# Down projection over 512 tokens with a collected remainder, weight work in both stages, and one split tile of 576 columns per SiLU product

## The chip, the cores and the metric

One core of one Trainium2 chip. The metric is device time in microseconds (us), a median over runs. The kernel before takes 1488.43 us, the median of 3 runs that lie between 1488.2 and 1488.91.

## The reference

Three layers follow one another over 8 batches of 576 tokens, 4608 tokens in all, with a model width of 512.

```python
def sm_attn(qq, kk, vv):
    s = scale * np.matmul(qq, kk.transpose(0, 1, 3, 2))
    ...
    return np.matmul(a, vv)
p_packed = sm_attn(p, k, v)          # 32 packed rows for each head
out = sm_attn(q, p_packed, p_packed)
...
g = x @ w_gate                       # first MLP: 512 -> 1536 -> 512
silu = g * (1.0 / (1.0 + np.exp(-g)))
return (silu * (x @ w_val) @ w_out)
...
h = x @ w_in                         # second MLP: 512 -> 2048 -> 512
return (h * np.cos(h)) @ w_out
```

The attention has 8 heads of 64. Everything is float32 at the interface. The kernel gets near that with pairs: a value is split into a rounded part "hi" and the remainder "lo", both of the 4-byte type f32r, and a product is three matmuls, hi x hi, hi x lo and lo x hi (the list PASSES).

## The kernel before, in words

**Stages.** A block is one batch of 576 tokens. For each of eight blocks there is an up stage (`a_up`, L402 to L448) and a down stage (`a_down`, L478 to L499) of the first MLP. The attention of the next block runs in pieces between the matmul groups of the down stage. The second MLP follows over all 4608 tokens, from DRAM (`x2d`), in its own stage of 384 and 512 columns (L685, L700).

**Up stage.** It has 12 tiles f of 128 hidden units, and for each two halves c of 288 tokens. A half of blocks 1 to 7 has 12 matmuls of 288 columns into the banks `pg` and `pv` (L433). ScalarE takes SiLU of `pg` (L441), VectorE multiplies with `pv` into a tile `h` of 288 columns (L444), and a half later the product is split: ScalarE writes the hi part, VectorE the lo part of `g` (helper `split`, L86 and L87). The stationary operand `wp` is the gate and value weight already multiplied with the packed rows of the attention; its first four tiles are made and split in the down stage before (`a_wp`, step 6), so that the up stage's first matmuls wait for that split. In block 0 the up stage decodes weights of the first MLP as well.

**Down stage.** It has eight groups n = (o, c) of 36 matmuls of 288 columns: output tile o, token half c, 12 tiles f and three passes. Each group accumulates in one bank, which ScalarE evicts to `x2e` (L498) and sends to `x2d` by a DMA from its own queue (L499). Ahead of groups 0, 2, 3, 4, 5 and 6 stand the pieces of the next block's attention: `a_s1` (scores of the packed rows, with their softmax), `a_t` (transposes), `a_pp`, `a_ppt`, `a_s2` (second scores, with the softmax in two chains u of 576 columns) and `a_wp`.

**Weight work.** The weights of the second MLP come in a packed form. In blocks 1 to 6 each half of the up stage carries one step of their preparation (`extra`, L450 to L464): load, decode on ScalarE and VectorE, sums, a split, and a store to DRAM (`w2_load`, `w2_decode`, `w2_work`, `w2_store`). That makes 24 steps a block.

**Order.** The kernel is written under a manual schedule: each engine executes its instructions in the order in which the code issues them, and SP and ScalarE each issue DMAs in that order too. An engine that waits holds all that is queued behind it. Tiles come from pools with a fixed number of buffers: `ct` 18, `mt` 12, `ht` 11, and eight PSUM banks.

Of the kernel before, what the change touches and what calls it, by code (L numbers as in the profile page):

```python
# [22 lines left out]
NPAIR = H // 2  # L23
HS = S // 2
NC = -(-S // 128)
SPAD = 128 * NC
# [3 lines left out]
NG = NPF // 2  # L30
SBUFS, CBUFS = 11, 18
SIN_SCALE = 6.28318500518798828
# [8 lines left out]
def attention_mlp_kernel(ctx: ExitStack, tc: tile.TileContext, qT, kT, vP, pP, wgv, w1o, w2, out):  # L41
# [12 lines left out]

    x2d = dr.tile([KD, 128, NT], F32, name="x2d")
    w2u = dr.tile([NPF, 7, 128, 512], F32, name="w2u")
    w2d = dr.tile([NF2, 128, 2, 512], F32, name="w2d")
# [10 lines left out]
    def mt(shape, dt, name):  # L68
        return sb.tile(shape, dt, tag="m", name=name, bufs=12)

    def ht(shape, dt, name):
        return sb.tile(shape, dt, tag="s", name=name, bufs=SBUFS)
# [325 lines left out]
    def flush_split():  # L398
        while pend_split:
            pend_split.pop(0)()  # L400

    def a_up(b):  # L402
        g = []
        for f in range(NF1):
# [9 lines left out]
            if b == 0:  # L414
                for u in range(2):
                    for c in range(2):
                        for o, p_ in zip((0, 128), banks[c]):
                            PE.matmul(  # L418
                                out=p_, lhsT=w[:, u, o:o + 128], rhs=a2[u][:, HS * c:HS * c + HS],
                                start=(u == 0), stop=(u == 1),  # L420
                            )
                    if u == (f == 0) and f + 1 < NF1:
                        a_wp0(f + 1)
            for c in range(2):
                sl = slice(HS * c, HS * c + HS)
# [16 lines left out]
                flush_split()  # L442
                h_ = ht([128, HS], F32, "h")
                DVE.tensor_tensor(out=h_, in0=s_, in1=pv, op=ALU.mult)  # L444
                pend_split.append(lambda h_=h_, gt=gt, sl=sl: split(h_, gt[:, 0, sl], gt[:, 1, sl]))
                extra(b, f, c)
            prefetch(b, f)
        return g  # L448

    def extra(b, f, c):  # L450
        if b == 0:
            u_step(0, 1)
            u_step(1, 1)
            if f == 0:
                u_step(2, 1)
        elif b < B - 1:
            s_ = 24 * (b - 1) + 2 * f + c
            if s_ % 2 == 0 and s_ // 2 < 4 * NF2:
                w2_store()
                w2_load(s_ // 2 + 1)  # L460
                w2_work(2)
                w2_decode(s_ // 2)
            else:
                w2_work(1)  # L464

    def prefetch(b, f):
# [7 lines left out]
        if f == 9 and b == 0:  # L474
            for j in range(NPAIR):
                load_v(n, j)

    def a_down(b, g, steps):  # L478
        for n in range(8):
            for s_ in steps.get(n, ()):  # L480
                s_()
            if 0 < b < B - 1 and n == 0:
                for j in range(NPAIR):
                    load_v(b + 1, j)
            if b + 1 < B and n == (2 if b == 0 else 0):
                for j in range(NPAIR):
                    load_q(b + 1, j)
            o, c = n // 2, n % 2
            sl = slice(HS * c, HS * c + HS)
            acc = bank([128, HS], "o1")  # L490
            for f in range(NF1):
                for i, (x, y) in enumerate(PASSES):
                    PE.matmul(  # L493
                        out=acc, lhsT=wo[o, f // 4][:, x, f % 4, :], rhs=g[f][:, y, sl],
                        start=(f == 0 and i == 0), stop=(f == NF1 - 1 and i == 2),
                    )
            ev = ht([128, HS], F32, "x2e")
            ACT.activation(out=ev, in_=acc, func=AF.Copy)  # L498
            ACT.dma_start(out=x2d[o, :, S * b + HS * c:S * b + HS * c + HS], in_=ev)  # L499

# [51 lines left out]
    with tc.manual_schedule():  # L552
# [38 lines left out]
        for b in range(B):  # L591
# [4 lines left out]
            if b == 0:  # L596
                w2_load(0)
            n = b + 1
            steps = {}
# [239 lines left out]
```

## Time and profile before

| | before |
|---|---|
| median of 3 runs | 1488.43 us |
| profiled execution | 1488.04 us |
| its span, first to last instruction | 1486.3 us |
| TensorE matmuls busy | 1478.3 us, 99% |
| VectorE busy | 985.8 us, 66% |
| ScalarE busy | 839.4 us, 56% |
| granted TensorE clock, mean | 1.000 |
| DMA, mean over the span | 173 GB/s |

The span lies inside the profiled execution's time; 1.7 us stand around it. The down stages of the eight blocks begin at 83.5, 172.3, 260.8, 349.4, 437.6, 525.6, 613.5 and 700.2 us; the second MLP's stage begins at 738.4 us. PE means matmuls and PEld the loading of their stationary operands, which lies beside them. Matmuls are pipelined: the mean time of one in the profile is from its start to its end, and the next starts before that end.

### The profile page before, as it was taken

Reading aid. Unit: us, or ns where it says so; the run is one execution under the profiler, and the core shown is the slowest. Engines: PE = TensorE matmul, PEld = TensorE weight load, DVE = VectorE, ACT = ScalarE, POOL = GpSimd, SP = SyncE. Lnnn points to the kernel's source line nnn. Section 1 sums busy time; section 2 is a strip of 40 time slices with the busy share of each in tenths; the row PEclk is TensorE's granted clock in tenths of the full one; section 3 lists DMA queues with packets and bytes.
Section 4 is the critical chain, followed back from the end, with each engine's and each line's share of the span. In section 5 each row is a group of like instructions: output and inputs, shape, how many; then the busy total and the mean of one; then the engine's idle time right before and its main releaser. Section 6 shows DMA issues by size and latency. Waiting matters only on the chain.

```text
span 1486.3 us, 27615 instructions
## 1 busy us (share of the span) xinstructions
PE 1478.3 (99%) x10476; PEld 1338.7 (90%) x10476; DVE 985.8 (66%) x2048; ACT 839.4 (56%) x1917; POOL 3.0 (0%) x22
## 2 busy tenths in 40 slices
PE   9999999999999999999999999999999999999999
PEld 6689998999899998989989999999999999999997
DVE  6988749485673837355286866776686686677654
ACT  6986737375572736434284645656555564565642
POOL 0000000000000000000000000000000000000000
PEclk9999999999999999999999999999999999999999
DMA  8742616355162542201295586576667558556641
GB/s 328 260 156 86 239 46 226 117 173 195 52 194 75 161 136 89 80 22 43 92 393 178 181 288 197 178 241 204 215 191 256 180 180 290 195 179 195 206 161 43
DMA packets 129411, 257.14 MB, mean 173 GB/s; under 512 B 13568, under 2 KB 37120, under 8 KB 129280
## 3 DMA queue, kind: packets, MB, share of 16 engines
q1 hardware_dynamic: 120064, 245.94, 50.4%
q10 hardware_dynamic: 9216, 9.44, 1.8%
q8 instruction: 83, 1.36, 0.4%
q14 instruction: 48, 0.39, 0.1%
HBM read 213.39 MB, written 41.94 MB: 172 GB/s over the span
## 4 chain that ended last, share of the span: by engine, by line
PE 95%; DVE 2%; ACT 2%; DMA 1%; issue 0%; SPq 0%; ACTq 0%; DVEq 0%
PE acc L700 26%; PE p L685 23%; PE o L493 20%; PE pg L433 9%; PE pv L433 9%; PE wp L386 3%; PE pg L418 1%; PE pv L418 1%; PE pp L203 1%; PE s L229 1%; PE s L151 1%; PE wp L371 0%; DMA qt<-in_qT 0%; PE tp L192 0%; DMA vt<-in_vP 0%
## 5 line engine op out<-in xcount | busy, mean ns | idle before, releaser
L700 PE MATMUL acc<-wd,g 128*128 128x512 f32 x1728 | 413.8, 389 | 0.0
L685 PE MATMUL p<-xs,up 128*128 128x384 f32 x2016 | 372.9, 337 | 1.3 <-ACT p L760 1.3
L700 PEld LDWEIGHTS acc<-wd,g 128*128 128x128 f32 x1728 | 322.4, 188 | 57.1
L685 PEld LDWEIGHTS p<-xs,up 128*128 128x128 f32 x2016 | 353.7, 188 | 12.7 <-ACT p L760 1.6
L493 PEld LDWEIGHTS o<-g,wo 128*128 128x128 f32 x2304 | 306.7, 188 | 13.8 <-DVE d L250 5.0
L493 PE MATMUL o<-g,wo 128*128 128x288 f32 x2304 | 316.6, 296 | 0.3 <-DVE wo L87 0.2
L663 ACT ACTIVATE t<-c,quarter 128x384 f32<-128x384 f32 x144 | 88.4, 614 | 196.7 <-DVE c L773 191.0
L433 PE MATMUL pg<-a,wp 128*128 128x288 f32 x1008 | 162.4, 296 | 0.0
L433 PE MATMUL pv<-a,wp 128*128 128x288 f32 x1008 | 160.6, 294 | 0.0
L433 PEld LDWEIGHTS pg<-a,wp 128*128 128x128 f32 x1008 | 142.4, 188 | 11.7 <-ACT wp L86 8.4
L433 PEld LDWEIGHTS pv<-a,wp 128*128 128x128 f32 x1008 | 143.0, 188 | 0.0
L87 DVE TENSOR_TENSOR g<-h,g 128x288 fp32r<-128x288 f32 x192 | 87.5, 456 | 39.4 <-ACT g L86 39.2
L673 DVE TENSOR_TENSOR g<-t,g 128x384 fp32r<-128x384 f32 x192 | 106.0, 552 | 8.0 <-ACT g L660 7.8
L665 DVE TENSOR_TENSOR t<-t,k 128x384 f32<-128x384 f32 x192 | 106.1, 552 | 3.5 <-ACT k L669 1.8
L768 DVE TENSOR_TENSOR u<-v,p 128x384 f32<-128x384 f32 x48 | 26.6, 554 | 118.2 <-PE p L685 117.9
L441 ACT ACTIVATE silu<-pg 128x288 f32<-128x288 f32 x192 | 78.3, 408 | 42.0 <-PE pg L433 37.5
L666 ACT ACTIVATE t<-t 128x384 f32<-128x384 f32 x192 | 98.2, 512 | 2.6 <-DVE t L665 2.5
L498 ACT ACTIVATE x2e<-o 128x288 f32<-128x288 f32 x64 | 26.5, 413 | 128.3 <-PE o L493 127.9
L660 ACT ACTIVATE g<-t 128x384 fp32r<-128x384 f32 x192 | 98.5, 513 | 0.4 <-DVE t L671 0.4
L86 ACT ACTIVATE g<-h 128x288 fp32r<-128x288 f32 x192 | 85.0, 443 | 24.2 <-DVE h L444 23.8
L669 ACT ACTIVATE k<-t 128x384 int32<-128x384 f32 x192 | 98.2, 511 | 0.0
L444 DVE TENSOR_TENSOR h<-silu,pv 128x288 f32<-128x288 f32 x192 | 86.0, 448 | 16.1 <-PE pv L433 5.9
(95 smaller groups left out, 1346.9 us busy)
## 6 DMA issues: line engine op xcount, KB each, us to landing
up<-w2u SPq DMA_DIRECT2D x336, 256.0 KB, 3.2
wd<-w2d SPq DMA_DIRECT2D x96, 512.0 KB, 6.2
raw<-in_w SPq DMA_DIRECT2D x64, 256.0 KB, 3.2
w2u<-w2p SPq DMA_DIRECT2D x56, 256.0 KB, 2.2
raw<-in_wgv SPq DMA_DIRECT2D x24, 512.0 KB, 7.5
vt<-in_vP SPq DMA_DIRECT2D x32, 320.0 KB, 4.3
kt<-in_kT SPq DMA_DIRECT2D x32, 288.0 KB, 5.0
qt<-in_qT SPq DMA_DIRECT2D x32, 288.0 KB, 6.0
```

The source lines that it names most:

```text
L87: eng.tensor_tensor(out=lo, in0=src, in1=hi.bitcast(F32), op=ALU.subtract)
L433: PE.matmul(out=p_, lhsT=w[u][:, x, o:o + 128], rhs=a2[u][:, y, sl], start=(n == 0), stop=(n == 5),)
L444: DVE.tensor_tensor(out=h_, in0=s_, in1=pv, op=ALU.mult)
L493: PE.matmul(out=acc, lhsT=wo[o, f // 4][:, x, f % 4, :], rhs=g[f][:, y, sl], start=(f == 0 and i == 0), stop=(f == NF1 - 1 and i == 2),)
L660: ACT.activation(out=three["g"][:, 0, :], in_=three["t"], func=AF.Copy)
L663: ACT.activation(out=now["t"], in_=now["h"], func=AF.Identity, scale=1.0 / TWO_PI, bias=quarter)
L665: DVE.tensor_tensor(out=one_["t"], in0=one_["t"], in1=one_["k"], op=ALU.subtract)
L666: ACT.activation(out=one_["t"], in_=one_["t"], func=AF.Sin, scale=SIN_SCALE)
L669: ACT.activation(out=now["k"], in_=now["t"], func=AF.Copy)
L673: DVE.tensor_tensor(out=three["g"][:, 1, :], in0=three["t"], in1=three["g"][:, 0, :].bitcast(F32), op=ALU.subtract)
L685: PE.matmul(out=out, lhsT=w[:, u, 128 * k:128 * k + 128], rhs=x[:, v, k, :], start=(first and k == 0 and i == 0), stop=(last and k == 1 an ...
L700: PE.matmul(out=acc, lhsT=gs[p, a, t][:, x, o:o + 128], rhs=wd[j, f][:, y, :], start=(f == 0 and n == 0), stop=(f == 3 and n == 2),)
```

## The change

**The down stage** takes tokens 0 to 511 of a block in four groups of 36 matmuls of 512 columns (`down_group`), instead of eight groups of 36 of 288. The attention's pieces stand at the same eighths of the stage as before, which are now the beginnings and the middles of the groups. An accumulator is evicted in two halves of 256 columns, each with its own DMA.

**The remainder.** The last 64 tokens of a block's `g`, hi and lo, are stored to DRAM (`rest`), 24 transfers of 128 x 64 a block on SP's queue, in the down stage behind the first half group; in block 7 they are stored along the up stage. The collected strips of the eight blocks make one more window of 512 columns. It is loaded back in 24 transfers of 128 x 512 (`load_rest`) and multiplied by `a_rest` in front of block 7's own down stage.

**Weight steps.** Of a block's 24 steps 16 stay in the up stage (two of three halves) and eight move into the down stage, two in each group, ahead of the tiles f = 3 and f = 9.

**The SiLU product** of a tile f is one tile `h` of 576 columns in blocks 1 to 7, written in halves and split once a tile instead of twice. Block 0 is as before. The pools become `ht` 9 and `mt` 13.

```diff
@@ -22,13 +22,15 @@
 ...
 HS = S // 2
+WIN = 512
+REST = S - WIN
 NC = -(-S // 128)
 SPAD = 128 * NC
 TH = 384
 NCH = NT // (2 * TH)
 NPF = NF2 // 2
 NG = NPF // 2
-SBUFS, CBUFS = 11, 18
+SBUFS, CBUFS = 9, 18
 SIN_SCALE = 6.28318500518798828
 
 PI = float(np.pi)
@@ -53,6 +55,7 @@
     dr = ctx.enter_context(tc.tile_pool(name="dr", bufs=1, space=bass.MemoryType.DRAM))
 
     x2d = dr.tile([KD, 128, NT], F32, name="x2d")
+    rest = dr.tile([NF1, 2, 128, B, REST], F32, name="rest")
     w2u = dr.tile([NPF, 7, 128, 512], F32, name="w2u")
     w2d = dr.tile([NF2, 128, 2, 512], F32, name="w2d")
 
@@ -66,7 +69,7 @@
         return sb.tile(shape, dt, tag="c", name=name, bufs=CBUFS)
 
     def mt(shape, dt, name):
-        return sb.tile(shape, dt, tag="m", name=name, bufs=12)
+        return sb.tile(shape, dt, tag="m", name=name, bufs=13)
 
     def ht(shape, dt, name):
         return sb.tile(shape, dt, tag="s", name=name, bufs=SBUFS)
@@ -399,6 +402,8 @@
         while pend_split:
             pend_split.pop(0)()
 
+    gr = []
+
     def a_up(b):
         g = []
         for f in range(NF1):
@@ -421,6 +426,7 @@
                             )
                     if u == (f == 0) and f + 1 < NF1:
                         a_wp0(f + 1)
+            hw = mt([128, S], F32, "h") if b > 0 else None
             for c in range(2):
                 sl = slice(HS * c, HS * c + HS)
                 pg, pv = banks[c]
@@ -440,12 +446,32 @@
                 s_ = ht([128, HS], F32, "silu")
                 ACT.activation(out=s_, in_=pg, func=AF.Silu)
                 flush_split()
-                h_ = ht([128, HS], F32, "h")
+                h_ = hw[:, sl] if b > 0 else ht([128, HS], F32, "h")
                 DVE.tensor_tensor(out=h_, in0=s_, in1=pv, op=ALU.mult)
-                pend_split.append(lambda h_=h_, gt=gt, sl=sl: split(h_, gt[:, 0, sl], gt[:, 1, sl]))
+                if b == 0:
+                    pend_split.append(lambda h_=h_, gt=gt, sl=sl: split(h_, gt[:, 0, sl], gt[:, 1, sl]))
+                elif c == 1:
+                    pend_split.append(lambda h_=hw, gt=gt: split(h_, gt[:, 0], gt[:, 1]))
                 extra(b, f, c)
             prefetch(b, f)
+            if b == B - 1 and f > 0:
+                store_rest(b, f - 1, g[f - 1])
+                if f > 2:
+                    gr.append(load_rest(f - 3))
         return g
+
+    w2_n = [0]
+
+    def w2_step():
+        s_ = w2_n[0]
+        w2_n[0] += 1
+        if s_ % 2 == 0 and s_ // 2 < 4 * NF2:
+            w2_store()
+            w2_load(s_ // 2 + 1)
+            w2_work(2)
+            w2_decode(s_ // 2)
+        else:
+            w2_work(1)
 
     def extra(b, f, c):
         if b == 0:
@@ -453,15 +479,8 @@
             u_step(1, 1)
             if f == 0:
                 u_step(2, 1)
-        elif b < B - 1:
-            s_ = 24 * (b - 1) + 2 * f + c
-            if s_ % 2 == 0 and s_ // 2 < 4 * NF2:
-                w2_store()
-                w2_load(s_ // 2 + 1)
-                w2_work(2)
-                w2_decode(s_ // 2)
-            else:
-                w2_work(1)
+        elif b < B - 1 and (2 * f + c) % 3 < 2:
+            w2_step()
 
     def prefetch(b, f):
         n = b + 1
@@ -475,28 +494,68 @@
             for j in range(NPAIR):
                 load_v(n, j)
 
+    def store_rest(b, f, gt):
+        for i in range(2):
+            SP.dma_start(out=rest[f, i, :, b, :], in_=gt[:, i, WIN:S].bitcast(F32))
+
+    def load_rest(f):
+        if f < NF1 // 2:
+            r = [mt([128, B, REST], F32R, "gr") for _ in range(2)]
+        else:
+            both = ct([128, 2, B, REST], F32R, "gr")
+            r = [both[:, i] for i in range(2)]
+        for i in range(2):
+            SP.dma_start(out=r[i].bitcast(F32), in_=rest[f, i])
+        return r
+
+    def down_group(o, moving, steps, to, between=None):
+        acc = bank([128, WIN], "o1")
+        for f in range(NF1):
+            if f % (NF1 // 2) == 0:
+                for s_ in steps.get(2 * o + f // (NF1 // 2), ()):
+                    s_()
+            if between and f % 6 == 3:
+                between()
+            for i, (x, y) in enumerate(PASSES):
+                PE.matmul(
+                    out=acc, lhsT=wo[o, f // 4][:, x, f % 4, :], rhs=moving(f, y),
+                    start=(f == 0 and i == 0), stop=(f == NF1 - 1 and i == 2),
+                )
+        for h in range(2):
+            ev = ht([128, WIN // 2], F32, "x2e")
+            ACT.activation(out=ev, in_=acc[:, WIN // 2 * h:WIN // 2 * h + WIN // 2], func=AF.Copy)
+            to(o, h, ev)
+
     def a_down(b, g, steps):
-        for n in range(8):
-            for s_ in steps.get(n, ()):
-                s_()
+        def to(o, h, ev):
+            c0 = S * b + WIN // 2 * h
+            ACT.dma_start(out=x2d[o, :, c0:c0 + WIN // 2], in_=ev)
+
+        def loads(n):
             if 0 < b < B - 1 and n == 0:
                 for j in range(NPAIR):
                     load_v(b + 1, j)
             if b + 1 < B and n == (2 if b == 0 else 0):
                 for j in range(NPAIR):
                     load_q(b + 1, j)
-            o, c = n // 2, n % 2
-            sl = slice(HS * c, HS * c + HS)
-            acc = bank([128, HS], "o1")
-            for f in range(NF1):
-                for i, (x, y) in enumerate(PASSES):
-                    PE.matmul(
-                        out=acc, lhsT=wo[o, f // 4][:, x, f % 4, :], rhs=g[f][:, y, sl],
-                        start=(f == 0 and i == 0), stop=(f == NF1 - 1 and i == 2),
-                    )
-            ev = ht([128, HS], F32, "x2e")
-            ACT.activation(out=ev, in_=acc, func=AF.Copy)
-            ACT.dma_start(out=x2d[o, :, S * b + HS * c:S * b + HS * c + HS], in_=ev)
+            if b < B - 1 and n == 1:
+                for f in range(NF1):
+                    store_rest(b, f, g[f])
+
+        steps = {n: tuple(steps.get(n, ())) + (lambda n=n: loads(n),) for n in range(8)}
+        for o in range(KD):
+            down_group(o, lambda f, y: g[f][:, y, 0:WIN], steps, to, w2_step if 0 < b < B - 1 else None)
+
+    def a_rest(gr):
+        def to(o, h, ev):
+            half = B // 2
+            ACT.dma_start(
+                out=x2d[o].rearrange("p (b n) -> p b n", b=B)[:, half * h:half * h + half, WIN:S],
+                in_=ev.rearrange("p (b n) -> p b n", b=half),
+            )
+
+        for o in range(KD):
+            down_group(o, lambda f, y: gr[f][y].rearrange("p b n -> p (b n)"), {}, to)
 
     late = {}
 
@@ -595,6 +654,12 @@
             w2_store()
             if b == 0:
                 w2_load(0)
+            if b == B - 1:
+                for f in range(len(gr), NF1):
+                    if f == NF1 - 1:
+                        store_rest(b, f, g[f])
+                    gr.append(load_rest(f))
+                a_rest(gr)
             n = b + 1
             steps = {}
             if n < B:
```

The instructions of an engine stand in the written order. The three places below are in block 3's down stage and, for SP, at the program's change of stages; a number behind a name only tells one tile from another. `o` is an accumulator of the down projection, `tp`, `pp` and `ppt` are the transposes and products of the next block's attention.

TensorE, from block 3's first output of the down stage up to the second scores, before:

```order
L493 MATMUL o_5114<-g,wo 128x288 x36
L493 MATMUL o_5154<-g,wo 128x288 x36
L192 MATMUL tp<-ident,E 128x128 x10
L493 MATMUL o_5216<-g,wo 128x288 x36
L203 MATMUL pp<-vt,ET 32x64 x40
L493 MATMUL o_5302<-g,wo 128x288 x36
L219 MATMUL ppt<-ident,ppu 128x128 x2
L493 MATMUL o_5350<-g,wo 128x288 x36
```

The same stretch now:

```order
L520 MATMUL o_4505<-g,wo 128x512 x36
L195 MATMUL tp<-ident,E 128x128 x10
L520 MATMUL o_4649<-g,wo 128x512 x18
L206 MATMUL pp<-vt,ET 32x64 x40
L520 MATMUL o_4649<-g,wo 128x512 x18
L222 MATMUL ppt<-ident,ppu 128x128 x2
L520 MATMUL o_4778<-g,wo 128x512 x18
```

Between two pieces of the attention stand 18 matmuls of 512 columns where 36 of 288 stood, and an accumulator spans two pieces.

ScalarE, from the second softmax's last exponential to the split of the next block's first `wp`, before. `d` is a score chain, `a` the finished attention rows, `x2e` an evicted accumulator:

```order
L241 ACTIVATE d_5391<-d_5391 128x576
L244 ACT_TABLE_LOAD
L244 ACTIVATE warm<-quarter 128x1
L86 ACTIVATE a_5432<-af 128x576
L86 ACTIVATE a_5442<-af 128x576
L498 ACTIVATE x2e<-o_5445 128x288
L499 DMA x2d<-x2e 128x288
L86 ACTIVATE wp<-wp 128x512 x4
```

The same stretch now:

```order
L244 ACTIVATE d_4823<-d_4823 128x576
L247 ACT_TABLE_LOAD
L247 ACTIVATE warm<-quarter 128x1
L89 ACTIVATE a_4864<-af 128x576
L89 ACTIVATE a_4874<-af 128x576
L89 ACTIVATE w2p<-w2f 128x256
L526 ACTIVATE x2e<-o_4778 128x256
L532 DMA x2d<-x2e 128x256
L526 ACTIVATE x2e<-o_4778 128x256
L532 DMA x2d<-x2e 128x256
L89 ACTIVATE wp<-wp 128x512 x4
```

Ahead of the four `wp` there is one eviction with its DMA more, and in this block the split of a weight tile (`w2p`).

SP's queue, from the end of the first MLP to the second MLP's first loads, now. `gr` is a strip tile loaded back, `xb`, `up` and `wd` are the second MLP's inputs:

```order
L499 DMA rest<-g 128x64 x2
L508 DMA gr<-rest 128x512 x2
L499 DMA rest<-g 128x64 x2
L508 DMA gr<-rest 128x512 x6
L499 DMA rest<-g 128x64 x2
L508 DMA gr<-rest 128x512 x2
L577 DMA xb<-x2d 128x2x384 x4
```

Before, the loads of `xb` followed the last loads of the first MLP directly; now the strips of the last tiles are stored, and loaded, ahead of them.

## Rows read from the trace of the kernel before

**Rows 1.** The page, busy time of each engine.

```profile
PE 1478.3 (99%) x10476; PEld 1338.7 (90%) x10476; DVE 985.8 (66%) x2048; ACT 839.4 (56%) x1917; POOL 3.0 (0%) x22
```

**Rows 2.** By stretch: window, length, busy (instructions) by engine, clock, DMA share, GB/s.

```profile
349.40:393.86 44.46, 44.46 (x452) 41.81 (x446) 20.00 (x44) 16.38 (x38) 0.00 (x0) 1.00 0.34 111
393.86:437.60 43.74, 43.74 (x386) 39.69 (x384) 34.43 (x85) 33.62 (x87) 0.30 (x2) 1.00 0.50 153
```

**Rows 3.** TensorE's timeline, block 3: start, length, operation, count, [wait before, releaser].

```profile
349.44 9.80 PE L493 MATMUL o<-g,wo 128*128 128x288 f32 x72
...
376.21 1.20 PE L229 MATMUL s<-qt,ppT 64*32 64x288 f32 x32
...
384.21 9.81 PE L493 MATMUL o<-g,wo 128*128 128x288 f32 x72
393.86 0.95 PE L433 MATMUL pg<-a,wp 128*128 128x288 f32 x6
```

**Rows 4.** The page, groups: count, busy us, mean ns of one, idle before.

```profile
L700 PE MATMUL acc<-wd,g 128*128 128x512 f32 x1728 | 413.8, 389 | 0.0
...
L493 PE MATMUL o<-g,wo 128*128 128x288 f32 x2304 | 316.6, 296 | 0.3 <-DVE wo L87 0.2
...
L87 DVE TENSOR_TENSOR g<-h,g 128x288 fp32r<-128x288 f32 x192 | 87.5, 456 | 39.4 <-ACT g L86 39.2
```

**Rows 5.** TensorE's timeline, block 7's down stage and the program's end.

```profile
700.24 38.32 PE L493 MATMUL o<-g,wo 128*128 128x288 f32 x288
...
1455.34 27.36 PE L700 MATMUL acc<-wd,g 128*128 128x512 f32 x120
```

**Rows 6.** VectorE's timeline, end of block 3's and begin of block 7's down stage.

```profile
377.04 1.58 DVE L236 STREAM_TRANSPOSE d<-s 128x288 f32<-128x288 f32 x4 [10.29 <-PE s L229]
...
389.44 0.76 DVE L87 TENSOR_TENSOR a<-af,a 128x576 fp32r<-128x576 f32 x1 [0.81 <-ACT a L86]
390.74 2.48 DVE L87 TENSOR_TENSOR wp<-wp 128x512 fp32r<-128x512 f32 x4 [0.54 <-ACT wp L86]
...
701.82 0.46 DVE L87 TENSOR_TENSOR g<-h,g 128x288 fp32r<-128x288 f32 x1 [0.51 <-ACT g L86]
```

**Rows 7.** ScalarE's timeline, end of block 3's down stage.

```profile
388.73 0.69 ACT L86 ACTIVATE a<-af 128x576 fp32r<-128x576 f32 x1 [3.66 <-DVE af L252]
389.32 0.39 ACT L498 ACTIVATE x2e<-o 128x288 f32<-128x288 f32 x1
...
390.11 2.07 ACT L86 ACTIVATE wp<-wp 128x512 fp32r<-128x512 f32 x4 [0.40 <-ACT x2e L498]
```

**Rows 8.** SP's DMA issues in block 3's down stage.

```profile
354.38 2.00 SPq L132 DMA_DIRECT2D vt<-in_vP  x4
356.43 3.04 SPq L128 DMA_DIRECT2D qt<-in_qT  x4
365.87 0.33 SPq L91 DMA_DIRECT2D raw<-in_w  x1
```

**Rows 9.** Timelines of block 0's down stage: ScalarE, TensorE twice, VectorE.

```profile
93.23 0.51 ACT L171 ACTIVATE E<-s,nm 128x288 f32<-128x288 f32 x1
...
94.18 4.03 PE L493 MATMUL o<-g,wo 128*128 128x288 f32 x26
98.40 1.58 PE L493 MATMUL o<-g,wo 128*128 128x288 f32 x10 [0.20 <-DVE wo L87]
...
112.71 0.69 DVE L87 TENSOR_TENSOR wo<-wof,wo 128x512 fp32r<-128x512 f32 x1 [2.24 <-ACT wo L86]
```

**Rows 10.** The page, DMA issues: count, KB each, us from issue to landing.

```profile
up<-w2u SPq DMA_DIRECT2D x336, 256.0 KB, 3.2
...
qt<-in_qT SPq DMA_DIRECT2D x32, 288.0 KB, 6.0
x2d<-x2e ACTq DMA_DIRECT2D x64, 144.0 KB, 1.8
...
pt<-in_pP SPq DMA_DIRECT2D x8, 64.0 KB, 3.4
```

## The prediction

> **What bounds the kernel now.** I read the page's shares first. TensorE is busy 1478.3 of 1486.3 us [rows 1], so its time is the kernel's time: a change pays only where it shortens the list of matmuls, and costs only where it makes that list wait. Then the table by stretch. In the down stage of block 3 (349.40 to 393.86 us) and in the up stage behind it TensorE is busy throughout at a granted clock of 1.00, while VectorE has 20.0 of 44.5 us in the down stage and 34.4 of 43.7 in the up stage [rows 2]. So VectorE and ScalarE have no price of their own; what they do in front of a matmul that needs it has. The third view, TensorE's own timeline through one down stage, shows no bracket with a wait in it [rows 3]. The pace is read there: 72 matmuls of 288 columns take 9.80 us.
>
> **The matmuls.** One of 288 columns lasts 296 ns from start to end [rows 4], so 71 starts fill 9.80 - 0.30 = 9.50 us, 133.9 ns each. The last block's down stage, with nothing between, gives (38.32 - 0.30)/287 = 132.5 ns [rows 5]. For 512 columns the program's last 120 matmuls give (27.36 - 0.39)/119 = 226.6 ns [rows 4, 5]. The step between the two paces is 92.7 ns for 224 columns, 0.414 ns a column; what is left, about 14.5 ns, comes with every matmul whatever its width. The change keeps the columns (2304 x 288 = 1296 x 512) and drops 1008 matmuls. Before: 7 blocks x 288 x 133.9 + 288 x 132.5 ns = 308.1 us. After: 1296 x 226.6 ns = 293.7 us, made up of 32.6 us in each of eight blocks and 32.6 us for the collected remainder. Gain 14.4 us, the whole of what the change can win. By the widest reading of the rows, the page's busy time per matmul with its tails (413.8 us / 1728 = 239.5 ns [rows 4]), the new matmuls would take 310.4 us and lose 2.3.
>
> **What is beside the path.** The split of a block's product goes from 168 pairs of 288 columns to 84 of 576. VectorE had 456 ns for one of 288 and 0.76 us for one of 576 [rows 4, 6]; 168 x 0.456 - 84 x 0.76 = 13 us of its work go, and as much on ScalarE, but in up stages where TensorE never waited: nothing. The weight steps stay 24 a block; eight move into the down stage, where VectorE has 24 us free: nothing, except at the place below. The 24 strip stores of each block take SP about 0.45 us each (4 loads there take 2.0 us [rows 8]), 11 us of a queue that before has over 5 us with no issue in this stage (359.5 to 365.9 [rows 8]) and whose next load is not urgent: nothing, if a store lands as x2d's do.
>
> **First cost: the end of each down stage.** Here the cover goes. From the second score matmuls (376.21) to the first matmul of the next up stage (393.86) TensorE has 17.65 us of its own work [rows 3]. In that time the softmax runs on VectorE nearly without a gap, from 377.04 to the split of `a` that starts at 389.44; behind it ScalarE evicts one accumulator, issues its DMA, and only then splits the four `wp`; VectorE's halves of these run from 390.74, 0.6 us each [rows 6, 7]. The up stage's sixth matmul needs the second: ready at 392.0, 15.8 us after the start, wanted at 17.65 + 5 x 0.134 = 18.3. That is 2.5 us to spare. The change takes 108 matmuls of 288 columns in this stretch to 54 of 512: 14.46 to 12.24 us, so the sixth matmul is wanted at 16.1. And it lengthens the chain: an accumulator is now evicted in two halves with a DMA issue each, so one more eviction and issue stand before the `wp` split (389.32 to 390.11, 0.79 us [rows 7]); in blocks 3 to 5 a weight split too (some 0.3 us net). Ready at 16.6 to 16.9; with 0.1 us for the signal TensorE waits 0.6 us in blocks 1, 2 and 6 and 0.9 in 3 to 5: 4.5 us. Queued behind the late split on ScalarE are the next SiLU and the evictions; counted through to the fourth tile of the up stage they stay 0.4 us or more ahead of their matmuls, so the wait is paid once. From both sides: 0 a block if the chain starts earlier than I count, 2 if the weight decode ahead of the first transpose (0.5 us to spare by my count) runs late.
>
> **Second cost: block 0.** Its up stage is unchanged and leaves both engines behind. The exponentials of block 1 end at 93.74 [rows 9] and the transposes, which come 36 x 226.6 ns after 83.50, now want them at 91.7 to 92.9: 1.3 us. The copies of the transposes stand behind the same ScalarE work as before, decodes of `wo` and two evictions, so the next step waits 0.6, the one after 0.4. The last weight split of `wo` stands before the second softmax on VectorE; it was late at 112.71 for an eviction that now comes earlier, and is about 1.2 us late for a score matmul that comes 2 us earlier; then 0.6 as in other blocks. Against these 4.1 us stand 0.6 of waits that are there now and go (26 matmuls in 4.03 us where 3.6 would do, and a bracket of 0.20 [rows 9]). Cost 3.5 us, between 1 and 6.
>
> **Third cost: the remainder.** After the last up stage the collected product needs the last strip's way out and back: SiLU product and split behind the last matmul (about 2.3 us; VectorE's was done at 702.3, 2.0 us after 700.24, with 288 columns [rows 5, 6]), store (issue 0.4, landing 1.8), two loads of 256 KB (issue 0.4 each, landing 3.2 as `up` [rows 10]), and six loads queued ahead, so that the issues wait on one another. About 9.0 us; TensorE wants it after 33 matmuls, 7.5 us. Cost 1.5, between 0 and 5 (a landing of 6.0, as `qt` has [rows 10]). At the change of stages seven loads of weights are waited for as before, the last a microsecond later: 0.3.
>
> **The sum.** 14.4 - 4.5 - 3.5 - 1.5 - 0.3 = 4.6 us off the profiled execution's 1488.04 (its span of 1486.3 and 1.7 around it): 1483.4. The median shown is 0.4 above that execution, so I say 1484.0.
>
> **A rule against it.** The rows above leave 14.5 ns with each matmul. The Trainium skill (TensorE: Matmul & The Clock Gate, Back-to-back issue gap) gives a warm gap of N/2.4 + 2.5 ns for a matmul by itself. This case's trace differs: 133.9 against 122.5 at 288 columns, 226.6 against 215.8 at 512. By that rule the 1008 matmuls would be worth 2.5 us and the sum would be a loss of 7.3; the measurement decides.
>
> **Rivals.** (a) *The chain keeps up.* If ScalarE and VectorE, freed of a third of the weight steps in the up stage, take the softmax a microsecond faster, the first cost goes: 1479.5, or 1477.7 with half the second. Against it: the chain starts from a TensorE matmul, not from a backlog, and 13.2 of its 15.8 us are VectorE's own instructions with two waits of 0.8 for ScalarE. Chance 0.16.
> (b) *The stores hold ScalarE.* SP's and ScalarE's transfers take eight DMA semaphores in turn, and an issue waits until the transfer eight before has landed; ScalarE's DMA of the second accumulator waits for the 21st and 22nd strip. At 0.45 us a store these land two microseconds before. From 0.75 us each, a landing of 6 us, ScalarE stands at its DMA, and with it the copy that the score matmuls need; at 1 us a store about 1.1 us more in each of six blocks, 1490.5; at 1.5 some 27 us. For it: `pt`, 64 KB in short rows, took 3.4 us to land; against: x2d's rows took 1.8 [rows 10]. Chance 0.12, slower. The Trainium skill (DMA: Bandwidth & Descriptors, Specifications) asks for 512 bytes or more a descriptor and says that below it the DMA reads, modifies and writes; the strips have 256, and no run here shows a transfer of such rows alone.
> (c) *The waits are longer all along* (weight decode ahead of the transposes late by 0.7 us in six blocks, the round trip at 5): 14.4 - 8.7 - 4.5 - 5 - 0.3, 1492.5 at its worst and 1488 in the middle. Chance 0.14, mostly no change.
> (d) *The matmuls do not get cheaper*, for a pace near 235 ns with these operands, between the two readings above: 304.6 us instead of 293.7, gain 3.5 against costs of 9.8: 1494.7. The two stretches of 512 columns in the trace agree on 226.6, so 0.04, slower. The Trainium skill's rule would end near here, at 1495.7.
>
> **The numbers.** The forecast has 0.54; its own range is 1480.5 to 1487.5. About 0.2% (3 us) is what a measurement of this kernel can tell from no change, so faster means below 1485.5, slower above 1491.4. Of the forecast's 0.54 some 0.38 lie below 1485.5; with (a) 0.16 that is 0.54, and a little of (c): 0.55. Within: 0.16 and 0.10 of (c) and 0.03 of (b): 0.29. Slower: 0.16. Range 1477.5 to 1490.5; the upper parts of (b), (c) and (d) are left out.
>
> **What would show it.** Right: 1296 down matmuls at 226 to 227 ns; a bracket with a wait for the `wp` split at the first up matmul of blocks 2 to 7, 0.5 to 1 us each, no other wait inside blocks 2 to 6; two or three waits in block 0; one wait on `gr` in the collected product. Wrong: waits of the score matmuls for `ppT` or of ScalarE for a DMA in the down stages (b), no wait before the up stages (a), a pace above 230 ns (d), or waits inside an up stage, where I count none.

## The result: slower by 0.6%, and the profile after

The changed kernel takes 1497.87 us, the median of 4 runs from 1495.89 to 1499.7, against 1488.32 for the kernel before beside it (4 runs). The ratio is 1.0064 with a 95% interval of 1.0046 to 1.0081: slower, where a gain of 4 us was forecast. The execution shown here is the one of 1499.7 us, with a span of 1497.9.

The page's totals deceive. Its busy line (as [rows 1]) and the shares of the chain that ended last:

```profile
PE 1478.9 (99%) x9468; PEld 1279.0 (85%) x9468; DVE 981.5 (66%) x1964; ACT 829.4 (55%) x1841; POOL 3.0 (0%) x22
...
PE 87%; DVE 5%; ACT 3%; DMA 2%; SPq 1%; issue 1%; ACTq 0%; DVEq 0%
```

There are 1008 matmuls fewer, and TensorE is as busy as before, though it is also idle for 11 us more (19.0 us of the span for 8.0). Some matmuls must have become longer. And TensorE holds 87% of the chain, where it held 95% before.

Cut at the first down matmul of every block, the stages tell where. Lengths in us, of before, of the change, and of three experiments that come below:

| stage | before | changed | late stores | both repairs | wp first |
|---|---|---|---|---|---|
| to block 0's down stage | 83.50 | 84.17 | 83.14 | 82.99 | 83.22 |
| block 0 down, block 1 up | 88.79 | 87.93 | 86.41 | 86.42 | 84.99 |
| block 1 down, block 2 up | 88.54 | 83.17 | 83.17 | 83.15 | 83.06 |
| block 2 down, block 3 up | 88.61 | 83.17 | 83.17 | 83.16 | 83.76 |
| block 3 down, block 4 up | 88.21 | 84.15 | 83.47 | 83.46 | 82.85 |
| block 4 down, block 5 up | 87.94 | 86.46 | 83.48 | 83.49 | 82.85 |
| block 5 down, block 6 up | 87.94 | 87.70 | 83.48 | 83.49 | 82.87 |
| block 6 down, block 7 up | 86.72 | 81.91 | 81.93 | 81.92 | 81.44 |
| block 7 down, with the remainder | 38.16 | 70.67 | 71.41 | 65.31 | 65.31 |

The rows that begin in blocks 1, 2 and 6 come out within 0.5 us of the forecast of 5.3 us less. Those of blocks 3, 4 and 5 were to be 5.0 us shorter each and are 4.1, 1.5 and 0.2; that of block 0 was to be 2.4 shorter and is 0.9; the remainder costs more than forecast. The first row lies anywhere from 83.0 to 84.2 us in the profiles of all the runs. Behind the last row the second MLP takes 747.9 us before and 748.6 now. TensorE's timeline at the end of block 5's down stage (as [rows 3]):

```profile
539.90 8.45 PE L520 MATMUL o<-g,wo 128*128 128x512 f32 x36
550.93 0.53 PE L439 MATMUL pg<-a,wp 128*128 128x288 f32 x2 [2.57 <-ACT wp L89]
551.65 1.00 PE L439 MATMUL pg<-a,wp 128*128 128x288 f32 x4 [0.19 <-DVE wp L90]
```

The wait for the `wp` split stands where the prediction put it, but it is 2.6 us long. By stretch (columns as in [rows 2]), what follows it:

```profile
550.93:553.12 2.19, 2.00 (x11) 1.59 (x12) 2.19 (x4) 2.14 (x5) 0.00 (x0) 1.00 0.95 272
553.12:556.54 3.42, 3.42 (x17) 3.42 (x16) 1.46 (x4) 1.49 (x5) 0.00 (x0) 0.50 0.23 77
556.54:560.00 3.46, 3.46 (x32) 3.15 (x39) 2.56 (x6) 2.81 (x8) 0.00 (x0) 1.00 0.58 168
```

The granted clock is 0.50 for 3.42 us, the lower of TensorE's two levels (1.2 GHz), and 17 matmuls start there where the next 3.46 us have 32. This stands as busy time, so no wait shows it. The trace has three such stretches ahead of its last microsecond: at 464.4, behind a wait of 1.5 us before block 5's up stage, at 553.1, and at 689.7, behind the wait for the collected strips:

```profile
685.54 2.07 PE L520 MATMUL o<-gr,wo 128*128 128x512 f32 x5 [0.35 <-DMA gr<-rest]
689.67 27.18 PE L520 MATMUL o<-gr,wo 128*128 128x512 f32 x111 [2.06 <-DMA gr<-rest]
```

Why is the `wp` split of block 5 late? VectorE (as [rows 6]) begins the score transposes at 536.14. Their scores were done at 533.8, but a weight decode stands ahead:

```profile
535.34 0.42 DVE L108 SCALAR_TENSOR_TENSOR w2f<-w2t,w2f 128x256 uint32<-128x256 uint32 x1 [10.61 <-ACT w2f L102]
535.80 0.43 DVE L111 SCALAR_TENSOR_TENSOR w2f<-raw,w2f 128x256 uint32<-128x256 uint32 x1
536.14 1.57 DVE L239 STREAM_TRANSPOSE d<-s 128x288 f32<-128x288 f32 x4
```

ScalarE, which begins the decode, had waited 4 us for the load that it reads:

```profile
534.46 0.43 ACT L101 ACTIVATE w2t<-raw 128x256 f32<-128x256 f32 x1 [4.05 <-DMA raw<-in_w]
```

That load is issued at 530.30. SP's timeline (as [rows 8]) shows what stood before it:

```profile
512.95 0.65 SPq L94 DMA_DIRECT2D raw<-in_w  x1
513.65 15.94 SPq L499 DMA_DIRECT2D rest<-g  x24
529.68 0.53 SPq L366 DMA_DIRECT2D w2d<-w2p  x1
530.30 0.58 SPq L94 DMA_DIRECT2D raw<-in_w  x1
```

The list of SP's waits, over all blocks, names what the stores waited for among loads (us in all, times, longest):

```profile
SPq L499 <- DMA qt<-in_qT: 10.4, 16, 1.2
...
SPq L499 <- DMA vt<-in_vP: 5.1, 9, 0.8
```

The 24 strip stores take 15.9 us, not 11. The first eight need 8 us, one after another as the large loads ahead of them land; the rest go at 0.47 us each. The store itself is quick: the page has `rest<-g`, 32 KB, with 1.6 us to landing.

The stores stand in every block, yet only blocks 3 to 5 show the long wait. In blocks 1 and 2 the load behind them is issued 19.2 and 19.0 us after the stage's start, in blocks 3 to 5 after 19.9, 21.2 and 21.2; its decode waits 0.2 and 0.4 us for it there, and 1.4, 2.9 and 4.0 here. Block 6 has no such load.

### The profile page after: what moved, and what is told of

It is laid out like the page before. It is cut to its first block, busy times and chain, and to the rows that moved or that the text cites. A ratio compares the mean times of both kernels' runs of the same rounds, so it can differ in the third digit from the quotient of the medians.

```text
span 1497.9 us, 25873 instructions
## 1 busy us (share of the span) xinstructions
PE 1478.9 (99%) x9468; PEld 1279.0 (85%) x9468; DVE 981.5 (66%) x1964; ACT 829.4 (55%) x1841; POOL 3.0 (0%) x22
## 4 chain that ended last, share of the span: by engine, by line
PE 87%; DVE 5%; ACT 3%; DMA 2%; SPq 1%; issue 1%; ACTq 0%; DVEq 0%
PE acc L765 26%; PE p L750 22%; PE o L520 13%; PE pg L439 9%; PE pv L439 9%; PE wp L389 2%; PE pg L423 1%; PE pv L423 1%; DMA rest<-g 1%; DMA raw<-in_w 1%; SPq L499 1%; DVE af L255 1%; DMA raw<-in_w1o 1%; DVE d L253 1%; PE s L154 1%
## 5 line engine op out<-in xcount | busy, mean ns | idle before, releaser
L520 PE MATMUL o<-g,wo 128*128 128x512 f32 x1152 | 273.6, 394 | 0.0
L520 PEld LDWEIGHTS o<-g,wo 128*128 128x128 f32 x1152 | 213.2, 188 | 56.0 <-issue 6.0
L439 PE MATMUL pg<-a,wp 128*128 128x288 f32 x1008 | 167.8, 300 | 5.9 <-ACT wp L89 5.1
L90 DVE TENSOR_TENSOR g<-h,g 128x576 fp32r<-128x576 f32 (+1 forms) x108 | 74.4, 689 | 48.3 <-ACT g L89 48.1
L779 DVE TENSOR_TENSOR oacc<-oacc,acc 128x512 f32<-128x512 f32 x108 | 73.7, 683 | 32.2 <-PE acc L765 32.2
L526 ACT ACTIVATE x2e<-o 128x256 f32<-128x256 f32 x72 | 27.5, 382 | 111.3 <-PE o L520 96.5
```

The costliest lines, as they stand in the source:

```text
L439: PE.matmul(out=p_, lhsT=w[u][:, x, o:o + 128], rhs=a2[u][:, y, sl], start=(n == 0), stop=(n == 5),)
L520: PE.matmul(out=acc, lhsT=wo[o, f // 4][:, x, f % 4, :], rhs=moving(f, y), start=(f == 0 and i == 0), stop=(f == NF1 - 1 and i == 2),)
```

## The experiments

Theory A: SP's queue. The stores hold a weight load that the change moved behind them, and its decode holds the softmax. Theory B, the prediction's: one more eviction and a weight split ahead of the `wp` split. Each kernel was timed beside the kernel before, which took 1487.75 to 1487.99 in these runs.

**The stores later** (1489.62 us, 10 runs; 1.0009, 1.0000 to 1.0018).

```diff
-            if b < B - 1 and n == 1:
+            if b < B - 1 and n == 5:
                 for f in range(NF1):
                     store_rest(b, f, g[f])
```

> Against the changed kernel one thing differs: in blocks 0 to 6 the 24 strip stores are issued behind the second scores (step 5) instead of behind the first half group. Theory A (SP's queue): the stores hold the weight load behind them, its late decode stands ahead of the score transposes on VectorE, and so the whole softmax and the wp split are late. Then the waits before the up stages behind blocks 3, 4 and 5 (0.7, 1.7 and 2.8 us in the changed kernel) fall to 0.3 or less each, the two half-clock stretches of 3.4 us behind two of them go as well, and the time is 1488 to 1490. Theory B (what the prediction held: one more eviction and a weight split ahead of the wp split): the stores do not matter, the three waits stay as they are, 1496 to 1500.

The three long waits and both of their half-clock stretches are gone; the last stretch, in the remainder, stays. SP in block 5:

```profile
511.49 0.55 SPq L94 DMA_DIRECT2D raw<-in_w  x1
518.54 0.52 SPq L366 DMA_DIRECT2D w2d<-w2p  x1
519.11 0.60 SPq L94 DMA_DIRECT2D raw<-in_w  x1
519.76 12.23 SPq L499 DMA_DIRECT2D rest<-g  x24
```

VectorE's score transposes, and TensorE at the stage's end:

```profile
527.20 1.58 DVE L239 STREAM_TRANSPOSE d<-s 128x288 f32<-128x288 f32 x4 [1.36 <-PE s L232]
```

```profile
542.01 0.53 PE L439 MATMUL pg<-a,wp 128*128 128x288 f32 x2
542.73 1.00 PE L439 MATMUL pg<-a,wp 128*128 128x288 f32 x4 [0.19 <-DVE wp L90]
```

The load for that decode now goes 15.7 us ahead of the transposes (511.49) where it went 5.8 us ahead, and VectorE waits for TensorE again, by 1.36 us. The table gives the price of the stores' place: 1.5 us in block 0, 0.7, 3.0 and 4.2 in blocks 3 to 5, 9.4 together. That is read from the slowest of the changed kernel's four executions; by the medians the late stores save 8.3 us. Theory A holds for these.

**The stores in pairs** (1488.87 us, 10 runs; 1.0008, 0.9998 to 1.0017).

```diff
-        for i in range(2):
-            SP.dma_start(out=rest[f, i, :, b, :], in_=gt[:, i, WIN:S].bitcast(F32))
+        SP.dma_start(out=rest[f, :, :, b, :].rearrange("i p n -> p i n"), in_=gt[:, :, WIN:S].bitcast(F32))
```

> The changed kernel with hi and lo strip of a tile in one store: 12 of 64 KB a block instead of 24 of 32 KB, same bytes and rows of 256 bytes, same place. If SP's time goes with the number of issues (0.47 us each once the transfers ahead have landed, and some 8 us for the first eight, which wait for eight large loads), the stores end after about 10 us instead of 16 and the weight load lands 6 us earlier: the three waits go, 1488 to 1491. If it goes with the bytes or the rows of 256 bytes, the stores still end at 15 us or later and the time stays at 1495 or more.

In block 5 the twelve stores take 9.75 us (507.47 to 517.2), and the same waits go. It is the number of issues and the loads ahead of them, not the bytes.

**All weight steps in the up stage** (1497.76 us, 4 runs; 1.0070, 1.0054 to 1.0087).

```diff
-        elif b < B - 1 and (2 * f + c) % 3 < 2:
+        elif b < B - 1:
             w2_step()
...
-            down_group(..., steps, to, w2_step if 0 < b < B - 1 else None)
+            down_group(..., steps, to)
```

> The changed kernel with all 24 weight steps of a block in the up stage again, as before the change; strip stores stay where they are. Theory A: no weight load stands behind the stores any more, so the three waits go as with the late stores: 1488 to 1491, if the up stages carry 24 steps without a wait as they did before the change. Theory B: only the one weight split of 0.4 us ahead of the wp split goes; waits of 0.3, 1.3 and 2.4 us stay, 1495 or more.

Half a miss. No long wait stands before the up stages of blocks 3 to 5 any more, as A has it, but the time did not fall: the scores behind the up stages wait instead. TensorE at the end of block 2's up stage:

```profile
255.58 1.16 PE L154 MATMUL s<-kt,pt 64*32 64x288 f32 x16 [0.19 <-DVE h L450]
257.41 0.71 PE L154 MATMUL s<-kt,pt 64*32 64x288 f32 x14 [0.67 <-DVE h L450]
```

ScalarE, and then VectorE, at one tile's split before:

```profile
249.97 0.69 ACT L89 ACTIVATE g<-h 128x576 fp32r<-128x576 f32 x1 [1.02 <-DVE h L450]
```

```profile
250.69 0.76 DVE L90 TENSOR_TENSOR g<-h,g 128x576 fp32r<-128x576 f32 x1 [0.42 <-ACT g L89]
```

ScalarE waits for VectorE's product, then VectorE for ScalarE's hi part; a tile takes 3.7 us (the next split is at 253.68) and TensorE needs 3.2. Theory C: this is the price of the single split.

**The same with two splits** (1493.03 us, 4 runs; 1.0038, 1.0023 to 1.0053).

```diff
-                h_ = hw[:, sl] if b > 0 else ht([128, HS], F32, "h")
+                h_ = ht([128, HS], F32, "h")
...
+                pend_split.append(lambda h_=h_, gt=gt, sl=sl: split(h_, gt[:, 0, sl], gt[:, 1, sl]))
```

> The kernel with all 24 weight steps in the up stage, with the SiLU product split in two halves again as before the change. Theory C: splitting once a tile makes ScalarE and VectorE wait for each other in series (3.7 us a tile in that run's up stage, against 3.2 us of matmuls), so with 24 steps the up stages of the blocks with weight sums end 2.2 us late at the next scores. Then those waits go and the time is 1492 to 1494. Rival: the strip stores or the loads cause them, and they stay: 1496 or more.

4.7 us come back by the medians. The sizes of the pools `ht` and `mt` go back with the split, here and, the other way round, in the next run; these two do not part them from it. In the profiles the stages that begin in blocks 0 to 2 lost 5.8 us to the changed kernel when all steps stood in the up stage, and 3.0 of these come back. Waits of 0.7 us at the scores behind the up stages of blocks 2 and 3 stay, so C is about half of the cause there; the rest was not followed up.

**The single split alone, on the kernel before** (1491.45 us, 9 runs; 1.0026, 1.0016 to 1.0036). The edit is the same lines the other way round.

> The kernel before with only the single split tile of 576 columns (pools 9 and 13 as in the change): down stage and weight steps as before. Theory C: 1 to 2.2 us lost at the scores behind each of two to four up stages, 1490 to 1495, slower than before. What the prediction held: 13 us less work for VectorE beside the path, no change, 1488.

Slower by 3.7 us. The stages that begin in blocks 0 to 2 grow by 1.0 to 1.2 us each, and the scores that end them wait 0.3, 0.7 and 0.7 us for `h`. By itself this part of the change is a loss.

**The remainder later** (1491.86 us, 6 runs from 1488.48 to 1494.85; 1.0025, 1.0012 to 1.0038).

```diff
-                a_rest(gr)
...
         for o in range(KD):
+            if b == B - 1 and o == 1:
+                a_rest(gr)
             down_group(...)
...
-                steps = {0: (lambda: load_x2(0),)}
+                steps = {2: (lambda: load_x2(0),)}
```

> The changed kernel with the collected remainder behind the first group of block 7's own down stage instead of ahead of it, and the second MLP's input loads and sums one group later. Both theories: the waits for the strips (0.35 and 2.1 us) and the half-clock stretch behind them (1.7 us) go, since 8.2 us of matmuls lie over the round trip: 4 us less than the changed kernel, or 3 if the later sums cost a microsecond at the change of stages. The waits of blocks 3 to 5 stay.

TensorE through block 7's down stage:

```profile
674.32 8.35 PE L520 MATMUL o<-g,wo 128*128 128x512 f32 x36
682.50 32.80 PE L520 MATMUL o<-gr,wo 128*128 128x512 f32 x144
715.14 24.64 PE L520 MATMUL o<-g,wo 128*128 128x512 f32 x108
```

65.3 us without a wait instead of 70.7, 5.4 gained. That is more than the 4 expected: besides the waits of 2.4 us with a bracket and the slow stretch (1.7) there were short gaps without one. The waits of blocks 3 to 5 were to stay. In this profile they are 0.2, 1.5 and 1.2 us, without a slow stretch behind the last, though nothing in the edit touches them: with the stores early these waits vary from run to run.

**Both repairs** (1483.80 us, 8 runs; 0.9973, 0.9963 to 0.9983). Late stores and late remainder together.

> The late strip stores and the remainder behind the first group of block 7's down stage, together. If the two losses are separate, the stage lengths of the two runs add: the profile of the late stores (1489.7) less the 6.1 us by which block 7's down stage shrank in the other (71.4 to 65.3) gives 1483.6, no half-clock stretch but the last, clearly faster than before. If the transfers of one get into the way of the other, 1487 or more.

The two losses add as the table has them; no half-clock stretch is left but in the last microseconds. Beside the late remainder the late stores are worth 8.1 us by the medians (1491.86 to 1483.80), nearly as much as alone.

**The wait filled** (18 small matmuls: 1488.98 us, 10 runs; 1.0009, 0.9999 to 1.0018. Ten: 1487.84 us, 11 runs; 1.0001, 0.9992 to 1.0010). Both stand on the late stores.

```diff
+            if isinstance(between, tuple) and f == between[0]:
+                between[1]()
...
-            down_group(o, ..., {}, to)
+            down_group(o, ..., {}, to, (11, lambda: keep_busy(10)) if o == 0 else None)
```

> The kernel with the late strip stores, with 18 small matmuls on constants (about 2 us) put into the collected remainder's first group ahead of tile 11, where TensorE waits 2.2 us for the strips. If the wait is what drops the clock, the half-clock stretch of 3.4 us behind it goes and the time falls by about 1.7 us from 1489.6, to 1488, though TensorE does no useful work in that place. If the drop has another cause, it stays, 1489 to 1490.

> The same as the run with the filled wait, with 10 small matmuls instead of 18. There 18 made 36 instructions of 109 ns, 3.9 us, longer than the wait of 2.2 us that they were to fill, and so cost what they saved. Ten take 2.2 us. If the clock follows the wait, no half-clock stretch is left and the time is that of the late stores' runs that stayed at a clock of 1.000 (1487.6 to 1488.0). If filling only trades one cost for another, 1489 again.

TensorE where it waited, with 18 and with ten:

```profile
668.38 8.75 PE L523 MATMUL o<-gr,wo 128*128 128x512 f32 x33
676.97 4.18 PE L118 MATMUL wm<-zero 128*128 128x128 f32 x36
```

```profile
676.17 2.39 PE L118 MATMUL wm<-zero 128*128 128x128 f32 x20
```

Neither trace has a half-clock stretch here. With 18 the filler was longer than the wait and cost most of what it saved. With ten the kernel is 1.8 us faster than without, though not one useful matmul was moved. The late stores' ten runs say the same: the two at a mean clock of 1.000 took 1487.58 and 1488.00, those at 0.997 to 0.999 took 1488.55 to 1490.07. Of the runs with the filler 18 of 21 have a mean clock of 1.000, and none is below 0.999.

**Half the width** (1493.82 us, 4 runs; 1.0040, 1.0026 to 1.0054), on both repairs.

```diff
+        for h in range(2):
+            hs = slice(WIN // 2 * h, WIN // 2 * h + WIN // 2)
...
-                    out=acc, lhsT=..., rhs=moving(f, y),
+                    out=acc, lhsT=..., rhs=moving(f, y)[:, hs],
```

> The kernel with both repairs, with the down projection in groups of 256 columns instead of 512: 2592 matmuls for 1296, the same columns. It doubles the disputed term. If 14.5 ns come with every matmul, as the paces at 288 and 512 columns gave, 1296 more cost 18.8 us, less some 3 us since one eviction less stands ahead of the wp split: 1499 to 1503. If the number of matmuls were not what the change's gain comes from, 1481 to 1484.

10.0 us more, where 15 to 19 were expected. TensorE in block 7:

```profile
683.36 34.72 PE L521 MATMUL o<-gr,wo 128*128 128x256 f32 x288
```

Matmul follows matmul at 120.0 ns here, against 226.7 for 512 columns. Twice 120.0 less 226.7 is 13.3 ns for a matmul more, so the fixed part exists and is 13.3, not 14.5: 1296 x 13.3 = 17.3 us. Given back are 5.3 us ahead of the up stages (first 48 matmuls in 6.45 us again, one eviction less ahead of the split). The 2 us that remain lie in the stages that the attention's pieces cut: there 512-column matmuls follow one another at 228 ns on average, not 226.7, and 256-column ones at 119.9.

**The split ahead of the eviction** (1480.37 us, 5 runs; 0.9949, 0.9936 to 0.9963), on both repairs.

```diff
+        if o == 2 and steps.get(6):
+            pend_evict.append(evict)
+        else:
+            evict()
```

> The kernel with both repairs (late strip stores, remainder behind the first group), with the eviction of the third accumulator issued behind the wp split on ScalarE instead of ahead of it. In the repaired kernel the first 48 matmuls of an up stage take 6.9 us behind blocks 1 and 2 and 7.2 behind blocks 3 to 5, where before the change they take 6.44, and TensorE waits 1.0 us behind block 0. If the two-piece eviction ahead of the split is the cause, as the prediction had it, these fall to 6.4 to 6.5 and the wait of block 0 nearly goes: 3 to 4 us less than 1483.8, 1480 to 1481. Rival: the softmax's own end sets the split, nothing moves, 1484.

ScalarE at the end of block 4's down stage:

```profile
454.54 0.40 ACT L89 ACTIVATE w2p<-w2f 128x256 fp32r<-128x256 f32 x1
454.84 2.04 ACT L89 ACTIVATE wp<-wp 128x512 fp32r<-128x512 f32 x4
456.75 0.40 ACT L532 ACTIVATE x2e<-o 128x256 f32<-128x256 f32 x1
```

And TensorE:

```profile
448.74 8.45 PE L524 MATMUL o<-g,wo 128*128 128x512 f32 x36
457.03 0.95 PE L439 MATMUL pg<-a,wp 128*128 128x288 f32 x6
```

Six matmuls in one piece: the wait is gone, 3.4 us in all. Theory B was right about a real cost of 0.5 us in blocks 1, 2 and 6 and 0.8 in blocks 3 to 5, and A about what lay on top of it. In one up stage, block 3's, the first of the two groups of `wp` matmuls takes 2.9 us instead of 1.95; that was not followed up. This version is the fastest, 0.5% ahead of the kernel before.

**Both repairs with two splits** (1484.38 us, 11 runs; 0.9977, 0.9968 to 0.9985).

> The kernel with both repairs, with the SiLU product split in two halves again. With 16 weight steps in the up stage and 8 in the down stage, theory C leaves neither form a wait: 1483.8 within 0.5, the split tile is worth nothing here. Rival: the 13 us of work that the single split saves are needed, and the up stages fall behind without it: 1485.5 or more.

The medians are 0.6 us apart, just outside the 0.5 expected, and the stages from block 0's down stage on agree within 0.3 us. With 16 weight steps in the up stage the form of the split is worth nothing.

## Why the prediction was wrong

**The step that failed** is a sentence in "What is beside the path": the strip stores take SP 11 us of "a queue that before has over 5 us with no issue", "whose next load is not urgent: nothing". Both halves were wrong. The next load is that of a moved weight step, so the change itself made it urgent: with the eight moved steps four loads and four decodes a block came into this stage. And 11 us took the rate of loads in one place [rows 8] for all 24 stores. That eight transfers may be under way was used for ScalarE's DMA in rival (b) and not for SP's own stores, which stand right behind large loads. Cost: 9.4 us instead of 0 in the profiled execution, 3 of them half-clock time (the first 48 matmuls of the up stages of blocks 5 and 6 take 8.6 and 8.75 us where 7.2 do with late stores).

**The matmuls**: forecast 14.4, measured 9.7 (down matmuls of an undisturbed block 39.0 us before, 33.7 after, seven times; the last 38.2 against 65.3). The pace of 133.9 ns [rows 3] held the gaps where the work changes inside block 3's stage, that of 226.6 [rows 5] came from a stretch with none. Like with like, 132.5 and 226.7 ns, it is 11.5 us, and the wider matmuls lose 0.25 us more a block in the stages that the attention's pieces cut. The measured 120.0 and 226.7 ns differ by 106.7 for 256 columns and leave 13.3 with each matmul. The Trainium skill (TensorE: Matmul & The Clock Gate, Back-to-back issue gap) has, for a matmul by itself, 2.5 ns beside N/2.4; the trace agrees on the slope and not on the constant.

**The first cost** was right in place, cause and size where nothing else came in: 0.5 us found for 0.6, 0.8 for 0.9. In blocks 3 to 5 the late load came on top. Its mechanism was named under (c), weight decode ahead of the transposes, at 0.7 us each; against the blocks without it the transposes begin 0.7, 1.6 and 2.7 us late.

**An unseen gain.** The prediction has "up stages where TensorE never waited". In the kernel before it did wait behind three of them. The scores behind the up stages of blocks 2, 3 and 4 lasted 1.80, 1.86 and 1.47 us before, and 1.20 now; here of block 3, before and after:

```profile
347.64 1.86 PE L151 MATMUL s<-kt,pt 64*32 64x288 f32 x32
```

```profile
337.31 1.20 PE L154 MATMUL s<-kt,pt 64*32 64x288 f32 x32
```

That gives back 1.5 us that no term had. It comes with the moved weight steps: with all 24 in the up stage these scores wait in either form of the split, with 16 in neither. The agreement in the stages from block 1 and 2 rests on it: 0.7 us less from the matmuls than forecast, 0.6 more from here.

**Block 0**: 3.5 forecast. With the stores out of the way the stage is 2.4 us shorter, as forecast; with them 0.9. The places of the waits were right (`tp` 0.46, `pp` 0.25, the scores 1.64, `wp` 0.46 and 0.20 us). The cause given for the longest, a late split on VectorE, was not: a load of `wo` stood behind the stores too, and ScalarE waited for it ahead of the copy `ppT` that the scores need. With the late stores this wait is gone.

```profile
106.03 0.69 ACT L101 ACTIVATE dec<-raw 128x512 f32<-128x512 f32 x1 [2.23 <-DMA raw<-in_w1o]
```

**The remainder**: 1.5 forecast, 5.4 measured. The wait with brackets was 2.4, within the bounds given. What was missed is the clock: 1.7 us at half speed behind the wait, in this profile. No term had a price for what a wait does to the matmuls after it.

**Rival (b)** had the right culprit, the stores, on the wrong engine. A store landed in 1.6 us. ScalarE waited for a store three times in all, 0.5 us at the longest, and in blocks 1 to 6 no matmul waited for the copy behind it; its longest waits for a DMA are for weight loads. The rows of 256 bytes did no visible harm. **Rival (d)** falls as a mechanism, since the pace in a stretch without a change is 226.7. In size it is not far off: with the changes of work between them, 144 matmuls of a block take 33.7 us, 234 ns each, where (d) had 235. **The split** at nothing holds beside spread weight steps, as the last experiment shows. Alone it costs 3.7 us: a saving of an engine's work can lengthen the chain through it.

**The account.** The profiled execution was forecast at 1483.4 us and took 1499.7. Of the 16.3 between them 9.4 are the stores, 4.7 the matmuls and 3.9 the remainder. The other terms take 1.7 off: the unseen gain (1.5), the first cost (0.7) and block 0 without the stores (0.6), against 1.1 more in the first row and the second MLP.

Both repairs give 1483.8 us, where 1484.0 was forecast for the change itself. That is luck: the matmul term was 4.7 too high, and as much came back in small terms, the 1.5 of the remainder that went with its repair and the 1.5 of the unseen gain among them.

## What to carry to other kernels

Here DMAs issued in front of a load delayed it by the number of issues and by the transfers still under way, not by their bytes: before a queue's work is called free, follow the next load on it to its reader. A wait of two microseconds of TensorE cost nearly twice its length here, so look at the granted clock behind each wait before the loss is put down to the wait alone. And a change of several parts is priced with all of them in place: the single split is harmless only beside the spread weight steps, and those steps are harmless only if their loads are not held by two dozen stores.

## What was not expected of the hardware

Waits of about the same length had different ends. Over all the runs' traces, behind waits of 1.5, 2.1, 2.2 and 2.6 us the clock was 0.50 for 3.41 us; behind waits of 1.2, 1.3, 1.6 and 1.8 us it stayed at 1.00, and of ten runs of the late stores, whose profile has the wait of 2.2 us, two kept a mean of 1.000. The length of the wait alone does not decide it, and what else does no run here shows. With that fits that the changed kernel's four runs spread over 3.8 us, while the eight of both repairs, without such a wait, lie within 1.2. The Trainium skill (TensorE: Matmul & The Clock Gate, HAM oscillation) describes matmuls that start cold after a wait for a DMA, of 3 to 5 us in its example. The rows agree on the cold start, with 427 ns a matmul of 512 columns in the slow stretch against 227 outside, and show it behind shorter waits. In the one place where it was tried, a filler on constants was worth 1.8 us as long as it was no longer than the wait; moving useful matmuls there, as the late remainder does, was worth 5.8.
